# FFN input turned by VectorE instead of TensorE, in a DeltaNet and SwiGLU kernel

## The chip, the cores and the metric

The kernel runs on one NeuronCore of a Trainium2 chip. The core has a matrix engine (TensorE, PE in the profile, with its weight loads as PEld), a vector engine (VectorE, DVE), a scalar engine (ScalarE, ACT), GpSimd (POOL) and SyncE (SP, which here only issues transfers). They run side by side and wait for each other by semaphores. Each engine takes its instructions strictly in the order in which the kernel records them. The metric is the device time in microseconds.

## What is computed

A DeltaNet attention over 4 batches, 8 heads, 768 positions and head size 48 is followed by a SwiGLU feed-forward network (FFN) of 384 to 1536 to 384 channels. All is in fp32; the inputs of the weights come as 64-bit numbers, which the kernel converts itself.

```python
def _attn_ref(q, k, v, beta):
    k_n = k / (np.linalg.norm(k, axis=-1, keepdims=True) + 1e-06)
    for t in range(S):
        y[:, :, t] = np.einsum('bhd,bhde->bhe', q[:, :, t], state)
        v_old = np.einsum('bhde,bhd->bhe', state, kt)
        state = state + bt[:, :, :, None] * np.einsum('bhd,bhe->bhde', kt, vt - v_old)
# bridge: (B,H,S,D) -> (B*S, H*D)
def _moe_ref(x, w_gate, w_val, w_out):
    g = x @ w_gate
    silu = g * (1.0 / (1.0 + np.exp(-g)))
    return (silu * (x @ w_val)) @ w_out
```

## The kernel before

The sequence is cut into 12 chunks of 64 positions. A chunk goes through the recurrence in matrix form (`advance`): with Z, the inverse of a triangular matrix made of K, beta and K, come `p_r`, `p_u` and `uu`, then the new state and Y. Y of a chunk lies in SBUF with two batches times 64 positions on the partitions and, twice (`bp`), 384 channels along the free axis. The FFN's products want the channels on the partitions, so Y is turned into `x_ffn` (`xts[c]`). Before, TensorE does this by six products with the identity and ScalarE copies the result out of PSUM:

```python
        y = work.tile([128, NB, NJ, 2, D], FP32, name="y", tag="r", bufs=2)
        for bp in each:
            nc.scalar.copy(y[:, bp, :, 0], p_y[:, 0, bp])
            for b in range(2):
                nc.scalar.copy(y[half_of(b), bp, :, 1], p_y[half_of(1 - b), 1, bp])
        yield

        y_f = y.rearrange("p bp j par d -> p bp (j par d)")
        xts[c] = ffn_pool.tile([128, KT, TOK], FP32, name="x_ffn")
        p_f = ps_pair("p_f", "py")[:, :, 0 : KT * 128]
        p_f = p_f.rearrange("p bp (t n) -> p t bp n", t=KT)
        for bp in range(NB):
            for t in range(KT):
                at = slice(t * 128, (t + 1) * 128)
                nc.tensor.transpose(p_f[:, t, bp], y_f[:, bp, at], ident)
        x_v = xts[c].rearrange("p t (bp n) -> p t bp n", bp=NB)
        for bp in each:
            nc.scalar.copy(x_v[:, :, bp], p_f[:, :, bp])
        yield
```

The FFN of chunk c runs while the recurrence of chunk c+1 is put between its products. The main loop shows how: `gate_val` makes two of the twelve slices of the FFN's width, `fill(n)` records n further steps of the inversion that yields Z (VectorE's `substitute`, then transposes), and `point(c + 1)` records one step of the recurrence of the next chunk, or the turning of K and Q for a later one. `finish(c + 1)` records what is still left of the next chunk.

```python
        for c in range(2, NCH):
            for f in range(0, FT, 2):
                point(c + 1)
                gate_val(c, f, fill)
            point(c + 1)
            if c >= FAST:
                output_fast(c, fill)
            ...
            finish(c + 1)
```

```python
    def gate_val(c, f, fill, within=None):
        for w_sb, name in ((wg_sb, "p_gate"), (wv_sb, "p_val")):
            ...                       # 6 products of 128x256 into each of two halves
            if name == "p_gate":
                nc.scalar.activation(sil, ps[name], ACTF.Silu)
                fill(2)
        nc.vector.tensor_tensor(out=hs[c, f], in0=sil, in1=ps["p_val"], op=ALU.mult)
        if c >= FAST:
            if f >= FT // 2:
                sums_of_h(c, f)       # three sums or differences of h on VectorE
        fill(3)

    def turned(c, of_q, tag=None):
        ...
        if c >= blocks_of[of_q][1]:   # later chunks of K and Q: VectorE turns 32x32 blocks
            nc.vector.transpose(xt, blocks.rearrange("p bp h d -> p (bp h d)"))
            ...

    def output_fast(c, fill):
        ...                           # the output product in seven block products (chunks 3 to 11)
        product(1, 0, lambda f: h_of(c, f, 1), lambda f: w_t3[:, f])
        add(o[1][:, right], o[0][:, right], p[1, 0])
        fill(2)
        point(c + 1)
        product(0, 0, lambda f: h_of(c, f + FH, 0), quarter(1, 0))
        nc.scalar.copy(o[0][:, left], p[0, 0])
        for f in range(0, FH, 2):
            minus(h_of(c, f + FH, 0), h_of(c, f + FH, 0), s_of(2, f))
        product(1, 1, lambda f: s_of(1, f), lambda f: w_t1[:, f])
        add(o[1][:, right], o[1][:, right], p[1, 1])
        point(c + 1)
        ...                           # product(1, 0) again, then the last one:
        product(1, 1, lambda f: h_of(c, f + FH, 0), quarter(1, 1))
```

In the start, VectorE clears two tiles, the loads follow in the order given here, and the first inversion is made of the diagonal blocks of K's Gram matrix:

```python
        nc.vector.memset(zb, 0.0)
        nc.vector.memset(ztp[0], 0.0)
        ...
        for n in range(4):
            stage(n)                  # pieces of the weights
        load_q(0)
        load_k(2)
        load_k(3)
        ...
        first_diag(1, 0, p_g[1], copy_a)
        r_b = first_n()               # 1 / (norm + 1e-6), from GpSimd's power
        first_diag(1, 1, p_g[1], copy_v)
        nc.vector.transpose(mb.rearrange("p j i -> p (j i)"), first_of["flat"])
```

Of the kernel before, what the change touches and what calls it, by code (L numbers as in the profile page):

```python
# [14 lines left out]
C = 64  # L15
DP = 64
R = 32
# [4 lines left out]
def kernel(  # L22
# [25 lines left out]
    nc = tc.nc  # L48
# [4 lines left out]
    NB = B // 2  # L53
    DM = H * D
    DFF = moe_w_gate.shape[1]
    KT = DM // 128
    FT = DFF // 128
    NG = NCH // 2
    HH = NB * H
# [10 lines left out]
    def ps_pair(name, tag):  # L70

        return psum.tile([128, 2, 512], FP32, name=name, tag=tag, bufs=1)
# [17 lines left out]
    def slot(c):  # L90
        return c if c < AHEAD else (c - AHEAD) % (AHEAD - 1)
# [5 lines left out]
    ident = const.tile([128, 128], FP32, name="ident")  # L97
# [5 lines left out]
    ztp = [const.tile([128, 2, HH, C], FP32, name=f"zt{i}") for i in range(ZB)]  # L103
# [10 lines left out]
    def halves(x, c, bp, b):  # L114
        return x[2 * bp + b, :, c * C : (c + 1) * C, :]
# [9 lines left out]
    def load_q(c):  # L125
        for bp in range(NB):
            for b in range(2):
                nc.sync.dma_start(
                    out=qpad[c % QB][64 * b : 64 * b + 64, bp, :, 0:D],
                    in_=halves(q, c, bp, b).rearrange("h p d -> p h d"),  # L130
                )
# [198 lines left out]
    kt, qt, a_sb, a_of, p_sb, xts = {}, {}, {}, {}, {}, {}  # L330
# [3 lines left out]
    def half_of(x):  # L334
        return slice(64 * x, 64 * x + 64)
# [13 lines left out]
    def norms(c):  # L349

        ksq = work.tile([128, NB, H, D], FP32, name="ksq", tag="r", bufs=2)
        x = knp[c][:, :, :, 0:D]
        nc.vector.tensor_tensor(out=ksq, in0=x, in1=x, op=ALU.mult)
        n = n_t[0][:, c].rearrange("p (par bp j) -> p par bp j", par=2, bp=NB)
        ksq_v = ksq.rearrange("p bp (j par) d -> p par bp j d", par=2)
        for to, of, par in (
            (slice(0, 128), slice(0, 128), 0),
            (half_of(0), half_of(1), 1),
            (half_of(1), half_of(0), 1),
        ):  # L360
            nc.vector.tensor_reduce(
                out=n[to, par], in_=ksq_v[of, par], axis=mybir.AxisListType.X, op=ALU.add
            )
        n = n_t[0][:, c]
        nc.gpsimd.tensor_tensor(out=n, in0=n, in1=half[:, 0:HH], op=ALU.pow)
# [18 lines left out]
    def first_n():  # L384
        n = n_t[0].rearrange("p c h -> p (c h)")
        nc.vector.tensor_scalar_add(n, n, 1e-6)
        r_n = work.tile([128, R], FP32, name="r_n", tag="n_b", bufs=1)
        nc.vector.reciprocal(r_n, n)
        r_b = work.tile([128, R], FP32, name="r_b", tag="nb", bufs=1)
        nc.vector.transpose(r_b, r_n)  # L390
        return r_b
# [135 lines left out]
    def first_tiles():  # L527
        a = work.tile([128, C * 2 * HH], FP32, name="a_sb")

        first_of["flat"] = a[:, 0 : R * R]  # L530
        first_of["diag"] = a[:, 0 : R * R].rearrange("p (j h) -> p h j", j=R)
        a_sb[0] = a[:, R * R :].rearrange("p (c h j) -> p c h j", c=2, h=HH)
        zb = work.tile([128, R, R], FP32, name="zb", bufs=1)
        nc.vector.memset(zb, 0.0)
        nc.vector.memset(ztp[0], 0.0)
        first_of["zb"] = zb

    def first_gram(c, tag):
# [11 lines left out]
    def first_diag(c, par, p, copy):  # L550
        at = HH * c + HH // 2 * par
        copy(first_of["diag"][:, at : at + HH // 2], p[1][:, par, 1])
# [177 lines left out]
    def advance(c):  # L730

        kn = knp[slot(c)]
        zt = ztp[c // 2 % ZB][:, c % 2]
        zt = zt.rearrange("p (par bp j) i -> p par bp j i", par=2, bp=NB)
        if c > 0:
            scale_v(c)
        r = vin.pop(c)
        p_y = recur(ps_pair("p_y", "py"))
        if c > 0:
            p_r = recur(ps_pair("p_r", "px"))  # L740
            for bp, j, par, b, first in every():
                nc.tensor.matmul(  # L742
                    p_r[half_of(b ^ par), par, bp, j],
                    kt[c][half_of(par), bp, j, b],
                    state[half_of(par), b, bp, j],
                    start=first,
                    stop=True,
                    skip_group_check=True,
                )
            for bp, j, par, b, first in every():  # L750
                nc.tensor.matmul(  # L751
                    p_y[half_of(b ^ par), par, bp, j],
                    qt[c][half_of(par), bp, j, b],
                    state[half_of(par), b, bp, j],
                    start=first,
                    stop=False,
                    skip_group_check=True,
                )
            nc.vector.tensor_tensor(out=r, in0=r, in1=p_r, op=ALU.subtract)  # L759
        yield  # L760
        p_u = recur(ps_pair("p_u", "px"))
        for bp, j, par, b, first in every():
            nc.tensor.matmul(  # L763
                p_u[half_of(b), par, bp, j],
                zt[half_of(b ^ par), par, bp, j],
                r[half_of(b ^ par), par, bp, j],
                start=first,
                stop=True,
                skip_group_check=True,
            )  # L770
        uu = work.tile([128, 2, NB, NJ, D], FP32, name="uu", tag="r", bufs=2)
        each = range(NB) if c == 0 else (slice(0, NB),)
        for bp in each:
            nc.scalar.copy(uu[:, :, bp], p_u[:, :, bp])
        if c + 2 < NCH:
            load_v(c + 2)
        yield
        pq = p_sb.pop(c)

        def p_of_u():  # L780
            for bp, j, par, b, first in every():
                nc.tensor.matmul(  # L782
                    p_y[half_of(b ^ par), par, bp, j],
                    pq[half_of(b), par, bp, j],
                    uu[half_of(b), par, bp, j],
                    start=(c == 0 and first),
                    stop=True,
                    skip_group_check=True,
                )

        def of_state():
            p_s = recur(ps_pair("p_s", "px"))
            for bp, j, par, b, first in every():
                nc.tensor.matmul(  # L794
                    p_s[half_of(par), b, bp, j],
                    kn[half_of(b), bp, 2 * j + par],
                    uu[half_of(b), par, bp, j],
                    start=first,
                    stop=True,
                    skip_group_check=True,  # L800
                )
            if c > 0:
                nc.vector.tensor_tensor(out=state, in0=state, in1=p_s, op=ALU.add)
            else:
                nc.scalar.copy(state, p_s)
            for later in range(AHEAD, NCH):
                if freed_by_k(later) == c:
                    load_k(later)

        if 0 < c < NCH - 1:  # L810
            of_state()
        p_of_u()
# [6 lines that stand above are left out]

        y_f = y.rearrange("p bp j par d -> p bp (j par d)")  # L820
        xts[c] = ffn_pool.tile([128, KT, TOK], FP32, name="x_ffn")
        p_f = ps_pair("p_f", "py")[:, :, 0 : KT * 128]
        p_f = p_f.rearrange("p bp (t n) -> p t bp n", t=KT)
        for bp in range(NB):
# [7 lines that stand above are left out]
        if c == 0:  # L832
            of_state()
            yield
# [299 lines left out]
    with tc.manual_schedule(  # L1134
# [14 lines left out]

        nc.vector.memset(places[0][:, 0:1], 0)  # L1150
        norms(1)
        for n in range(4):
            stage(n)
        load_q(0)
        load_k(2)
        load_k(3)
        for n in range(4, 10):
# [5 lines left out]
        copy_a, copy_v = nc.scalar.copy, nc.vector.tensor_copy  # L1163
        turned(0, False)
        turned(1, False, "py")
        p_g = [first_gram(0, "px"), first_gram(1, "py")]
        first_diag(0, 0, p_g[0], copy_a)
        first_diag(0, 1, p_g[0], copy_v)
        copy_a(beta_b, beta_s.rearrange("p (g r) -> p g r", g=NG)[:, :, 0:R])
        first_diag(1, 0, p_g[1], copy_a)  # L1170
        r_b = first_n()
        first_diag(1, 1, p_g[1], copy_v)
        mb = new_mb()
        nc.vector.transpose(
            mb.rearrange("p j i -> p (j i)"), first_of["flat"]
# [121 lines left out]
```

## Time and profile before

The time before is 738.33 us, the median of three runs (738.02 to 739.34). The profiled execution spans 737.5 us.

| row of the profile | count | busy us | mean ns of one |
|---|---|---|---|
| L847 products `p_gate` and `p_val` | 1728 | 204.4 + 198.5 | 387 and 379 |
| L959 and L876 products `p_o` | 900 | 182.8 | 326 to 499 |
| L827 transposes `p_f` of Y | 72 | 10.6 | 286 |
| L830 copies `x_ffn` of 128x768 | 11 | 8.8 | 798 |
| L510 and L516 substitution | 372 | 63.3 + 63.7 | 340 and 343 |
| L862 `h_f` | 71 | 48.6 | 684 |
| L422 turning of K and Q by VectorE | 15 | 18.3 | 1216 to 1240 |

A line such as `L862 DVE ...` names the source line, the engine, the operation, what it writes and what it reads, with partitions x elements. In the timeline the first number is the start in us, the second the length. The chain of waits follows the work that ended last back to the start and gives, for each piece, its start and length. The busy time of an engine says how long its instructions ran, not whether something waited for them.

### The profile page before, as it was taken

The page shows a single profiled execution, that of the slowest core. Times are in us where ns is not written, and L with a number is a line of the kernel's source. Part 1 is how long each engine was busy: PE and PEld are TensorE (multiplying, and loading weights), DVE is VectorE, ACT ScalarE, POOL GpSimd, SP SyncE. Part 2 cuts the span into 40 slices and gives each one's busy share as a digit, 9 for nine tenths or more (in the row PEclk, how much of TensorE's full clock was granted, in tenths as well). Part 3 has the DMA queues.
Part 4 walks back from the last instruction along what each step waited for, and adds up shares of the span by engine and source line. Part 5 has one row for each costly group of instructions (what it writes and reads, how often), then busy time and mean ns, then how long its engine had stood idle before and what let it go on. Part 6 is the DMA issues. An engine that isn't in the chain of part 4 may idle for free.

```text
span 737.5 us, 22478 instructions
## 1 busy us (share of the span) xinstructions
PE 697.5 (95%) x10132; PEld 604.7 (82%) x10132; DVE 473.1 (64%) x977; ACT 154.7 (21%) x287; POOL 66.9 (9%) x46
## 2 busy tenths in 40 slices
PE   4657899999999999999999999999999999999997
PEld 3546788866787788988988988988988988989987
DVE  5999988978498163678854678854578853313122
ACT  3455443302401112011012011012011012021010
POOL 7008100201200000030000030000030000000000
PEclk9556999999999999999999999999999999999999
DMA  6775444121231012331302231302210100100000
GB/s 141 164 227 166 124 108 129 36 41 24 56 45 24 22 24 45 43 67 15 53 3 45 36 70 20 53 3 39 46 29 12 32 3 3 23 3 0 22 1 21
DMA packets 130735, 37.18 MB, mean 50 GB/s; under 512 B 122864, under 2 KB 125936, under 8 KB 130640
## 3 DMA queue, kind: packets, MB, share of 16 engines
q1 hardware_dynamic: 127184, 34.01, 22.7%
q10 hardware_dynamic: 3072, 1.57, 1.0%
q8 instruction: 79, 1.29, 0.7%
q0 software_dynamic: 384, 0.17, 0.1%
q14 instruction: 16, 0.13, 0.1%
HBM read 31.01 MB, written 4.72 MB: 48 GB/s over the span
## 4 chain that ended last, share of the span: by engine, by line
PE 83%; DVE 14%; issue 1%; DMA 1%; ACT 0%; ACTq 0%; SPq 0%; DVEq 0%
PE p_gate L847 23%; PE p_val L847 23%; PE p_o L959 17%; PE p_o L876 6%; DVE tmp L510 3%; PE p_g L444 3%; DVE zb L516 3%; PE p_u L763 2%; PE p_r L742 1%; PE p_s L794 1%; PE p_y L782 1%; PE p_y L751 1%; DVE last_h L287 1%; PE p_t L432 1%; DVE h_f L862 1%
## 5 line engine op out<-in xcount | busy, mean ns | idle before, releaser
L847 PE MATMUL p_gate<-x_ffn,wg_sb 128*128 128x256 f32 x864 | 204.4, 387 | 1.5 <-ACT x_ffn L830 1.5
L847 PE MATMUL p_val<-x_ffn,wv_sb 128*128 128x256 f32 x864 | 198.5, 379 | 0.0
L847 PEld LDWEIGHTS p_val<-x_ffn,wv_sb 128*128 128x128 f32 x864 | 163.8, 190 | 22.3
L847 PEld LDWEIGHTS p_gate<-x_ffn,wg_sb 128*128 128x128 f32 x864 | 161.1, 191 | 24.2 <-ACT x_ffn L830 2.0
L862 DVE TENSOR_TENSOR h_f<-sil,p_val 128x512 f32<-128x512 f32 x71 | 48.6, 684 | 147.5 <-PE p_val L847 147.0
L856 ACT ACTIVATE sil<-p_gate 128x512 f32<-128x512 f32 x72 | 43.0, 598 | 276.9 <-PE p_gate L847 247.3
L655 POOL TENSOR_TENSOR n_b<-mb,half 128x32 f32<-128x32 f32 x5 | 43.0, 8607 | 408.6 <-DVE mb L480 368.2
L959 PE MATMUL p_o<-wo_sb,h_f 128*128 128x192 f32 x432 | 75.6, 328 | 0.1
L959 PEld LDWEIGHTS p_o<-wo_sb,h_f 128*128 128x128 f32 x432 | 70.3, 190 | 1.2 <-DVE o_sb L969 0.7
L510 DVE TENSOR_TENSOR tmp<-zb,mb 128x31 f32<-128x31 f32 (+15 forms) x186 | 63.3, 340 | 12.2 <-PE p_j L630 6.8
L516 DVE TENSOR_TENSOR zb<-zb,tmp 128x31 f32<-128x31 f32 (+15 forms) x186 | 63.7, 343 | 6.5 <-DVE tmp L510 0.2
L969 DVE TENSOR_TENSOR o_sb<-o_sb,p_o 128x192 f32<-128x192 f32 x45 | 15.8, 350 | 53.4 <-PE p_o L959 36.2
L876 PE MATMUL p_o<-wo_sb,h_f 128*128 128x384 f32 x136 | 45.7, 490 | 0.0
L876 PEld LDWEIGHTS p_o<-wo_sb,h_f 128*128 128x128 f32 x136 | 25.3, 190 | 16.5
L959 PE MATMUL p_o<-last_k,h_f 128*128 128x192 f32 x180 | 32.2, 326 | 0.0
L959 PEld LDWEIGHTS p_o<-last_k,h_f 128*128 128x128 f32 x180 | 29.7, 190 | 0.0
L917 DVE TENSOR_TENSOR h_f<-h_f,h_f 128x256 f32<-128x256 f32 x54 | 22.4, 424 | 8.0 <-PE p_o L959 7.1
L959 PE MATMUL p_o<-last_h,h_f 128*128 128x192 f32 x144 | 26.3, 326 | 0.0
L959 PEld LDWEIGHTS p_o<-last_h,h_f 128*128 128x128 f32 x144 | 23.9, 190 | 0.0
L254 ACT ACTIVATE last_h<-last_h,rebias 128x512 int32<-128x512 uint32 (+2 forms) x26 | 15.3, 616 | 30.5 <-DVE last_h L246 30.4
L763 PEld LDWEIGHTS p_u<-vin,zt 64*64 64x64 f32 x768 | 13.7, 141 | 6.9 <-issue 3.2
L763 PE MATMUL p_u<-vin,zt 64*64 64x48 f32 x768 | 15.7, 228 | 2.4 <-DVE vin L759 1.2
(180 smaller groups left out, 692.6 us busy)
## 6 DMA issues: line engine op xcount, KB each, us to landing
vin<-in_v_dram SPq DMA_DIRECT2D x96, 48.0 KB
kn<-in_k_dram SPq DMA_DIRECT2D x40, 96.0 KB
out_dram<-o_sb SPq DMA_DIRECT2D x36, 96.0 KB
zt<-in_moe_w_out_dram SPq DMA_DIRECT2D x6, 384.0 KB
staged<-in_moe_w_out_dram SPq DMA_DIRECT2D x6, 384.0 KB
qpad<-in_q_dram SPq DMA_DIRECT2D x36, 64.0 KB
wo_sb<-in_moe_w_gate_dram SPq DMA_DIRECT2D x4, 512.0 KB
wo_sb<-in_moe_w_val_dram SPq DMA_DIRECT2D x4, 512.0 KB
```

The lines of the kernel that those rows point to most:

```text
L444: nc.tensor.matmul(p_v[par][half_of(b if of_q else b ^ par), bp, j], kt[c][half_of(par), bp, j, b], xt[half_of(par), bp, j, b],)
L510: nc.vector.tensor_tensor(out=t_v, in0=zb[:, 0 : j + 1, j : j + 1].to_broadcast([128, j + 1, m]), in1=mb[:, j : j + 1, j + 1 : R].to_broad ...
L516: nc.vector.tensor_tensor(out=zb[:, 0 : j + 1, j + 1 : R], in0=zb[:, 0 : j + 1, j + 1 : R], in1=t_v, op=ALU.add,)
L655: nc.gpsimd.tensor_tensor(out=n, in0=mb.rearrange("p j i -> p (j i)")[:, 0 : R * R : R + 1], in1=half, op=ALU.pow,)
L763: nc.tensor.matmul(p_u[half_of(b), par, bp, j], zt[half_of(b ^ par), par, bp, j], r[half_of(b ^ par), par, bp, j], start=first, stop=True, ...
L847: nc.tensor.matmul(ps[name][:, i], w_sb[:, t, (f + i) * 128 : (f + i + 1) * 128], xts[c][:, t], start=(t == 0), stop=(t == KT - 1),)
L856: nc.scalar.activation(sil, ps[name], ACTF.Silu)
L862: nc.vector.tensor_tensor(out=hs[c, f], in0=sil, in1=ps["p_val"], op=ALU.mult)
L876: nc.tensor.matmul(p_o, hs[c, f - f % 2][:, f % 2, bp * 128 : (bp + 1) * 128], wo_sb[:, f], start=(f == 0), stop=(f == FT - 1),)
L917: nc.vector.tensor_tensor(out=out, in0=a, in1=b, op=ALU.subtract)
L959: nc.tensor.matmul(p[x, part], a(f - f % 2)[:, f % 2], b(f), start=not begun and f == 0, stop=f == FH - 1, skip_group_check=True,)
L969: nc.vector.tensor_tensor(out=out, in0=a, in1=b, op=ALU.add)
```

## The change

From chunk 2 on, Y is turned by VectorE's transpose of 32x32 blocks straight from SBUF to SBUF: sixteen instructions per chunk, each taking 32 partitions of Y to 32 partitions of `x_ffn`. TensorE's six transposes, ScalarE's copy and the PSUM tile between them go away for these ten chunks. The aim is to take work from TensorE. The input needs no further step in between, as the loop over the 4 x 4 blocks does the exchange of the block rows.

Two smaller parts come with it. Z's first tile is cleared by ScalarE, which multiplies a repeated identity by zero, instead of VectorE's memset; and Q's first loads are issued ahead of the first four weight pieces. Besides, the second diagonal copy of VectorE is recorded ahead of the norm's steps.

```diff
         nc.vector.memset(zb, 0.0)
-        nc.vector.memset(ztp[0], 0.0)
+        nc.scalar.mul(
+            ztp[0].rearrange("p c h i -> p (c h i)").rearrange("p (n i) -> p n i", i=128),
+            ident[:, None, :].to_broadcast([128, 2 * HH * C // 128, 128]),
+            0.0,
+        )
...
         xts[c] = ffn_pool.tile([128, KT, TOK], FP32, name="x_ffn")
+        if c > 1:
+
+            y_q = y_f.rearrange("p bp (t q d) -> p q t bp d", t=KT, q=4)
+            x_q = xts[c].rearrange("p t (bp q n) -> p q t bp n", bp=NB, q=4)
+            for of_x in range(4):
+                for of_y in range(4):
+                    nc.vector.transpose(
+                        x_q[R * of_x : R * of_x + R, of_y],
+                        y_q[R * of_y : R * of_y + R, of_x],
+                    )
+            yield
+            return
         p_f = ps_pair("p_f", "py")[:, :, 0 : KT * 128]
...
         norms(1)
+        load_q(0)
         for n in range(4):
             stage(n)
-        load_q(0)
         load_k(2)
...
         first_diag(1, 0, p_g[1], copy_a)
+        first_diag(1, 1, p_g[1], copy_v)
         r_b = first_n()
-        first_diag(1, 1, p_g[1], copy_v)
         mb = new_mb()
```

## The prediction

> **What bounds the kernel now.** I read the page's shares and slices first, then the chain that ended last, then the timeline around each place where Y becomes the FFN's input x.
>
> ```profile
> PE 697.5 (95%) x10132; PEld 604.7 (82%) x10132; DVE 473.1 (64%) x977; ACT 154.7 (21%) x287; POOL 66.9 (9%) x46
> ...
> PE 83%; DVE 14%; issue 1%; DMA 1%; ACT 0%; ACTq 0%; SPq 0%; DVEq 0%
> ```
>
> TensorE bounds it. VectorE's 64% looks like room, but the share is an average. Before about 90 us VectorE carries the chain, and later it comes back in three short pieces. Here is the chain of work around one of them:
>
> ```profile
> 334.31 0.70 DVE h_f L862
> ...
> 338.70 0.42 DVE tmp L510
> ...
> 344.87 1.26 DVE kt L422
> 346.12 0.04 issue
> 346.17 1.16 PE p_g L444 x64
> ```
>
> From 334.31 to 346.12 the chain runs on VectorE without a hole (11.27 us busy of 11.90 by the window sums), and TensorE stands before `p_g` until `kt` is turned. The same stretch is on the chain at 445.4 to 457.2 and, ending in `qt`, at 556.5 to 568.3.
>
> What the change removes from TensorE is seen in the timeline near 408 us:
>
> ```profile
> 407.99 0.82 PE L827 MATMUL p_f<-ident,y 128*128 128x128 f32 x6
> 408.64 4.07 PE L959 MATMUL p_o<-wo_sb,h_f 128*128 128x192 f32 x24
> ```
>
> From the start of `p_f` to the start of the next product is 0.65 us: that is the price of the six transposes, not the 0.82 of their records, which overlap. Ten chunks make 6.5 us, the most that TensorE can gain.
>
> And the one x that is awaited (chunk 2), in the timeline:
>
> ```profile
> 191.78 0.80 ACT L830 COPY x_ffn<-p_f 128x768 f32<-128x768 f32 x1 [1.38 <-PE p_f L827]
> ...
> 192.63 2.86 PE L847 MATMUL p_gate<-x_ffn,wg_sb 128*128 128x256 f32 x12 [0.52 <-ACT x_ffn L830]
> ...
> 193.04 0.28 DVE L516 TENSOR_TENSOR zb<-zb,tmp 128x112 f32<-128x112 f32 x1
> ```
>
> **What the new instructions cost.** Their nearest kin in the groups by shape and the timeline:
>
> ```profile
> L688 DVE STREAM_TRANSPOSE z<-zt 32x256 f32<-32x256 f32 x16 | 6.1, 415 | 0.2
> L665 DVE STREAM_TRANSPOSE n_t<-n_b 128x32 f32<-128x32 f32 x5 | 1.1, 212 | 0.2
> ```
>
> [...] So a full turn of Y takes 4 x 4 instructions, each on 32 partitions and 192 elements (six blocks), and a quarter of the lanes. [...] the four L688 of one group start at 373.76, 374.13, 374.54 and 374.91, and the next instruction at 375.33. Where the quadrant stays, the step is 0.37 us; where it changes, 0.41 to 0.43, and nothing overlaps. In the new loop the input's quadrant changes at every instruction, so all are held. From 32 elements (212 ns) to 256 (433 ns for the held one) is 0.99 ns per element; 192 elements are 212 + 160 x 0.99 = 370 ns, plus 14 ns between two held ones, 0.385 us. Sixteen make **6.15 us of VectorE per chunk**, 61 us in all, against 0.65 us of TensorE and 0.80 us of ScalarE (L830) removed per chunk.
>
> **The change part by part.** In the built program's order the sixteen stand where the generator's step stands, so each place is worked out by itself.
>
> Chunk 2. They follow the substitution step that ends at 193.32 (L516 above), so x is ready at 193.32 + 6.15 + 0.1 = 199.55 where it was 192.58. The first `p_gate` waits for all sixteen: +6.95 us, all on the path.
>
> Chunk 3. y is ready at 235.6, VectorE is free from 241.8 and idle for 15.3 us up to 257.07, and x is needed at 251.5. Hidden; -0.65 us.
>
> Chunks 5, 7, 9. The sixteen stand between the substitution steps at 338.26 and 338.70, inside the stretch where VectorE is the chain. Everything behind shifts by 6.15 us: `kt` ends at 352.3 instead of 346.1, TensorE stands before `p_g`, and its 0.65 us come back as a longer wait. +6.15 us each, 18.45 us.
>
> Chunks 4, 6, 8. They start after the `o_sb` sum at 297.15 (chunk 4), at 297.5, and end at 303.65. Three differences of h (L917), which the last product reads, come next; TensorE, 0.65 us earlier, would reach that product at 302.81 and now waits for the first difference until about 304.15. `kt` then ends at 306.4 and `qt` at 307.5, against 303.2 and 304.3. The second `p_g` starts at 307.6 instead of 306.5, and `p_gate` at 308.65 instead of 307.52: +1.1 us each, 3.3 us.
>
> Chunk 10 has only `qt` to turn; the same reckoning from 629.2 gives +1.0 us. Chunk 11 (664 us): VectorE idles 5.8, 5.8 and 3.9 us before the `h_f` around it, so it has caught up before the `h_f` of 675.17; hidden, -0.65 us.
>
> The start. Z's clearing (1.76 us of VectorE at 2.45) is followed by 2.62 us of waiting for k, so its removal gains nothing; ScalarE has room between its table load (ends 4.9) and 7.97. Q's loads in front of the weights end TensorE's 2.36 us wait for `qpad` at 19.1, but VectorE's substitution is the path there. What matters is TensorE's stop in the middle of the first `p_g`, which the chain shows as
>
> ```profile
> 12.96 2.90 issue
> ```
>
> The trace doesn't say what it waits for. DMA share is 0.99 in that window, with the four weight pieces just issued. [...] If Q ahead of the weights shortens it, the norm's power on GpSimd (ends 16.17) becomes the limit and about 1.0 us is gained. If it stays, the 0.8 us of norm work that now stand behind the second diagonal copy go on the path. I take -0.3.
>
> Sum: 6.95 - 0.65 + 18.45 + 3.3 + 1.0 - 0.65 - 0.3 = **+28.1 us**, of which nothing is given back later, as TensorE bounds what lies between.
>
> The clock comes on top. In chunks 2, 5, 7, 9 TensorE now stands idle for some 7.4 to 8 us. [...] in windows of 3.41 us:
>
> ```profile
> 12.72:16.13 3.41, 0.51 (x54) 0.34 (x43) 0.57 (x1) 0.35 (x1) 3.41 (x2) 1.00 0.99 277
> 16.13:19.54 3.41, 1.05 (x46) 0.83 (x24) 2.83 (x7) 2.69 (x5) 0.79 (x4) 0.50 0.70 101
> 26.37:29.78 3.41, 3.41 (x125) 3.30 (x128) 3.13 (x9) 1.07 (x2) 0.00 (x0) 0.50 1.04 339
> 29.78:33.19 3.41, 1.21 (x79) 1.07 (x72) 3.17 (x8) 1.07 (x2) 0.00 (x0) 1.00 0.52 95
> ```
>
> The second number is TensorE's busy time, the one before the DMA share its granted clock: 0.51 us busy is followed by half clock, a full window by full clock. A stop of over 6.8 us holds one whole window. Half clock then lasts for the rest of the window of the restart (1.7 us on average) and one full window, 5.1 us, which costs half of that, 2.6 us. Four stops make 10 us; I take 8, since a small-tile window may count otherwise.
>
> 738.3 + 28.1 + 8 = **774 us**.
>
> **Rivals.** First: TensorE is the bound at 95% and VectorE has 36% free, so 6.5 us are gained, about 731 us. The shares speak for it; against it speaks the chain, which has VectorE at exactly the places where three of the ten blocks of sixteen land, and the awaited x of chunk 2. Second: the transposes overlap each other, as records of equal quadrants do, and cost 0.25 to 0.3 us, 4.5 us per chunk. Then chunk 2 costs 5.3, the three odd ones 13.5, the even ones give 0.5 each back: some +15 us, with the clock 760. Third: the stops come without the clock's fall[...]: 766.
>
> **Range and chances.** 757 to 785 holds the second and third rivals and a clock loss twice as large. Slower by over 2% begins at 753.1, just under the range: 0.91. Within 2% needs transposes of about 4 us and no clock loss: 0.06. Faster by over 2% (under 723.6) is more than removing all the transposes could give: 0.03.
>
> **What will show it.** Right: 160 transposes of 32x192 with a mean near 370 ns and steps near 0.385; VectorE near 530 us busy; waits of TensorE for `x_ffn` of some 7 us once and for `kt` or `qt` of 7 to 8 us three times, a new wait for h of about 1.3 us at the even chunks; slices of PEclk under 9 after 190, 350, 460 and 570 us. Wrong: steps under 0.3 us, `p_g` of chunk 5 less than 5 us later relative to the `p_val` before it, or a first `p_gate` of chunk 2 that doesn't wait for VectorE.

## The result, and the profile after

The changed kernel takes 779.15 us, the median of four runs (776.65 to 781.21), where the kernel before took 738.61 (738.02 to 739.34; the three runs of the first part and one more). The ratio is 1.0547, with a 95% interval of 1.0507 to 1.0586: slower. The profiled execution is the 776.65; it spans 774.9 us, 37.4 more than the one of before.

The page of the kernel after: busy times, the granted clock in slices, the shares of the chain that ended last, and the group of the new instructions.

```profile
PE 697.8 (90%) x10072; PEld 604.6 (78%) x10072; DVE 528.5 (68%) x1136; ACT 148.5 (19%) x278; POOL 67.7 (9%) x46
...
PEclk9657999999799999997999999999999899999999
...
PE 70%; DVE 25%; issue 2%; POOL 1%; DMA 1%; SPq 0%; DVEq 0%; ACT 0%
...
L832 DVE STREAM_TRANSPOSE x_ffn<-y 32x192 f32<-32x192 f32 x160 | 59.1, 369 | 2.0
```

TensorE has 60 products fewer and is busy for as long as before (697.8 against 697.5 us), because some of its products ran at half clock. Past the start the PEclk row shows it as two sevens and an 8 (chunks 2, 5 and 9); in chunk 7 the half clock lies across two slices, and both still show a 9. VectorE gained 55 us of work, and its part of the chain rose from 14% to 25%. TensorE's waits from 150 us to the end name the places (total us, times, longest):

```profile
PE p_g L444 <- DVE kt L422: 15.4, 3, 7.6
PE p_o L975 <- DVE o_sb L985: 8.1, 4, 2.0
PE p_g L444 <- DVE qt L422: 7.6, 1, 7.6
PE p_gate L863 <- DVE x_ffn L832: 7.3, 1, 7.3
```

There is one wait for x, in chunk 2, and there are four for an `o_sb` sum, one in each of chunks 4, 6, 8 and 10. Of the four for `kt` and `qt`, three are 7.6 us long (15.4 + 7.6 is three times 7.6 plus a remainder of 0.2); those belong to chunks 5, 7 and 9. The timeline of the kernel after in chunk 2 and in chunk 5 (start, length, and in brackets the wait of the first product):

```profile
192.78 6.11 DVE L832 STREAM_TRANSPOSE x_ffn<-y 32x192 f32<-32x192 f32 x16
198.94 5.39 PE L863 MATMUL p_gate<-x_ffn,wg_sb 128*128 128x256 f32 x12 [7.30 <-DVE x_ffn L832]
...
348.71 6.11 DVE L832 STREAM_TRANSPOSE x_ffn<-y 32x192 f32<-32x192 f32 x16
361.03 1.25 DVE L422 STREAM_TRANSPOSE kt<-qpad 128x1024 f32<-128x1024 f32 x1
362.33 1.99 PE L444 MATMUL p_g<-kt 64*64 64x64 f32 x64 [7.63 <-DVE kt L422]
```

Sixteen transposes take 6.11 us. Behind each stop the products run slowly: these twelve took 2.86 us before and take 5.39, and these 64 took 1.16 and take 1.99. The granted clock around chunk 2, in stretches of 3.41 us laid on the clock's steps (length, busy time of PE, PEld, DVE, ACT and POOL, granted clock, DMA share, GB/s):

```profile
190.45:193.86 3.41, 0.75 (x64) 0.64 (x64) 3.14 (x12) 1.63 (x3) 0.00 (x0) 1.00 0.77 158
193.86:197.27 3.41, 0.00 (x0) 0.00 (x0) 3.29 (x10) 0.00 (x0) 0.00 (x0) 0.50 0.20 37
197.27:200.68 3.41, 1.74 (x4) 1.47 (x5) 1.57 (x5) 0.00 (x0) 0.00 (x0) 0.50 0.00 0
200.68:204.10 3.42, 3.42 (x9) 2.71 (x9) 0.00 (x0) 0.00 (x0) 0.00 (x0) 0.50 0.00 0
204.10:207.51 3.41, 3.41 (x64) 2.79 (x64) 0.00 (x0) 0.60 (x1) 0.00 (x0) 1.00 0.00 0
```

To see where the 37.4 us arose, I compared the starts of the 72 `silu` activations (six per chunk) in the two traces. The table gives what each chunk lost or gained in all (+ is later than before); the clock's part is what the products behind a stop took beyond their former time.

| place | us | of which clock |
|---|---|---|
| start | -0.55 | |
| chunk 2 | +9.39, and +0.33 at its fourth pair of products | 2.53 |
| chunk 3 | -0.66 | |
| chunks 4, 6, 8, 10 | +1.62 each | |
| chunks 5, 7, 9 | +7.99, +7.38, +7.66 | 1.95, 1.35, 1.63 |
| chunk 11 | -0.66 | |
| sum | 37.4 | 7.46 |

### The profile page after: what moved, and what is told of

Its sections match the earlier page's. It is cut to its first block, busy times and chain, and to the rows that moved or that the text cites. A ratio compares the mean times of both kernels' runs of the same rounds, so it can differ in the third digit from the quotient of the medians.

```text
span 774.9 us, 22499 instructions
## 1 busy us (share of the span) xinstructions
PE 697.8 (90%) x10072; PEld 604.6 (78%) x10072; DVE 528.5 (68%) x1136; ACT 148.5 (19%) x278; POOL 67.7 (9%) x46
## 4 chain that ended last, share of the span: by engine, by line
PE 70%; DVE 25%; issue 2%; POOL 1%; DMA 1%; SPq 0%; DVEq 0%; ACT 0%
PE p_gate L863 22%; PE p_val L863 21%; PE p_o L975 13%; DVE x_ffn L832 6%; DVE tmp L510 4%; DVE zb L516 4%; PE p_g L444 3%; PE p_o L892 2%; PE p_u L767 1%; PE p_r L746 1%; PE p_s L798 1%; PE p_y L786 1%; PE p_y L755 1%; DVE h_f L933 1%; DVE h_f L878 1%
## 5 line engine op out<-in xcount | busy, mean ns | idle before, releaser
L863 PE MATMUL p_gate<-x_ffn,wg_sb 128*128 128x256 f32 x864 | 207.7, 391 | 8.2 <-DVE x_ffn L832 7.3
L863 PEld LDWEIGHTS p_gate<-x_ffn,wg_sb 128*128 128x128 f32 x864 | 163.6, 194 | 32.0 <-DVE x_ffn L832 7.4
L975 PE MATMUL p_o<-wo_sb,h_f 128*128 128x192 f32 x432 | 78.0, 335 | 8.1 <-DVE o_sb L985 8.1
L975 PEld LDWEIGHTS p_o<-wo_sb,h_f 128*128 128x128 f32 x432 | 72.7, 195 | 9.9 <-DVE o_sb L985 9.2
L510 DVE TENSOR_TENSOR tmp<-zb,mb 128x31 f32<-128x31 f32 (+15 forms) x186 | 63.3, 340 | 15.4 <-PE p_j L634 10.1
L832 DVE STREAM_TRANSPOSE x_ffn<-y 32x192 f32<-32x192 f32 x160 | 59.1, 369 | 2.0
L892 PEld LDWEIGHTS p_o<-wo_sb,h_f 128*128 128x128 f32 x136 | 25.4, 190 | 16.7
L444 PE MATMUL p_g<-kt 64*64 64x64 f32 x576 | 12.0, 241 | 15.4 <-DVE kt L422 15.4
L444 PEld LDWEIGHTS p_g<-kt 64*64 64x64 f32 x576 | 10.8, 154 | 18.0 <-DVE kt L422 16.6
```

Source lines behind the costliest of these rows:

```text
L444: nc.tensor.matmul(p_v[par][half_of(b if of_q else b ^ par), bp, j], kt[c][half_of(par), bp, j, b], xt[half_of(par), bp, j, b],)
L510: nc.vector.tensor_tensor(out=t_v, in0=zb[:, 0 : j + 1, j : j + 1].to_broadcast([128, j + 1, m]), in1=mb[:, j : j + 1, j + 1 : R].to_broad ...
L832: nc.vector.transpose(x_q[R * of_x : R * of_x + R, of_y], y_q[R * of_y : R * of_y + R, of_x],)
L863: nc.tensor.matmul(ps[name][:, i], w_sb[:, t, (f + i) * 128 : (f + i + 1) * 128], xts[c][:, t], start=(t == 0), stop=(t == KT - 1),)
L892: nc.tensor.matmul(p_o, hs[c, f - f % 2][:, f % 2, bp * 128 : (bp + 1) * 128], wo_sb[:, f], start=(f == 0), stop=(f == FT - 1),)
L975: nc.tensor.matmul(p[x, part], a(f - f % 2)[:, f % 2], b(f), start=not begun and f == 0, stop=f == FH - 1, skip_group_check=True,)
```

## The experiments

The theory: the sixteen cost what they take because each one waits for the one before; they cost time only where VectorE is the chain or x is awaited; and the long stops lower TensorE's clock besides. The rivals: the clock falls for another cause, the steps have nothing to do with the partitions read and written, or the smaller parts of the change carry some of the loss. All kernels are the changed kernel with the edit shown, so all of them hold the start's parts too. A set of chunks in an edit means that the others keep TensorE's transposes.

### Each place by itself

The start's parts alone, with Y turned by TensorE everywhere:

```diff
-        if c > 1:
+        if False:
```

> The changed kernel with Y turned by TensorE in all chunks again; only the parts at the start are kept (Q's loads ahead of the weights, Z cleared by ScalarE, the order of the second diagonal copy). Theory (the loss is VectorE's transposes, the start gives a little): the first silu comes 0.5 us earlier than before and nothing else moves, 738.6 - 0.55 = 738.0 us. Rival (the start parts carry a good part of the 40 us, for instance by late weights): over 745 us. Rival (the start gives the most of what was meant): under 735 us.

739.53 us in 13 runs, ratio 1.0005 [0.9997, 1.0013], where 738.0 was expected. The -0.55 of the two traces doesn't stand out from the scatter of the start: in the thirteen traces of kernels with this same start, the last `silu` of chunk 1 comes 0.08 to 1.15 us earlier than in the one trace of before. Clearing Z by ScalarE and loading Q ahead make no difference that the 13 runs show.

Only chunks 3 and 11:

```diff
-        if c > 1:
+        if c in (3, 11):
```

> VectorE turns Y in chunks 3 and 11 alone, the two where VectorE idles; start parts kept. Theory (what a transpose block costs depends on what stands behind it on VectorE): 0.66 us gained in each, 738.0 - 1.3 = 736.7 us, no half clock after 70 us. Rival (sixteen VectorE instructions cost their 6.1 us wherever they stand): 738.0 + 12.2 - 1.3 = 749 us.

737.63 us in 19 runs, ratio 0.9979 [0.9972, 0.9986]. In the trace, -0.65 and -0.66 us: where VectorE idles, the whole price of TensorE's six transposes is gained.

Only chunks 5, 7 and 9:

```diff
-        if c > 1:
+        if c in (5, 7, 9):
```

> VectorE turns Y in chunks 5, 7 and 9 alone, at the place of the changed kernel; start parts kept. Theory: three stops of TensorE before p_g, 6.0 us each without the clock and 1.3 to 2.6 us by half clock after each, 738.0 + 18.1 + 4 to 8 = 760 to 764 us. Rival (chunk 2 and the even chunks make most of the loss): under 750 us.

762.14 us, ratio 1.0317 [1.0301, 1.0332], inside the expected 760 to 764. The three chunks lose 6.88, 7.57 and 8.55 us, so the mechanism needs none of the other places. The clock's part (0.84, 1.53 and 2.51 once 6.04 is taken off) differs from that in the changed kernel (1.95, 1.35 and 1.63); the stops lie otherwise against the stretches of 3.41 us, which I take for the cause.

Only chunks 4, 6, 8 and 10:

```diff
-        if c > 1:
+        if c in (4, 6, 8, 10):
```

> VectorE turns Y in chunks 4, 6, 8 and 10 alone, at the place of the changed kernel; start parts kept. Theory: 1.62 us lost in each as in the changed kernel's trace, no half clock, 738.9 + 6.5 = 745.4 us. Rival (the loss of the even chunks comes only with the stops of the odd ones around them): about 736 us.

748.03 us (745.56 to 748.89), ratio 1.0118 [1.0101, 1.0136], 2.6 above what was expected. The profiled execution, the 745.56, has +1.62 or +1.63 in chunks 6, 8 and 10 and +2.76 in chunk 4. There, TensorE stands 1.18 us ahead of `p_gate`, and the profile gives no releaser ("issue"). The other three runs are 2 to 3 us longer and left no trace, so what they lost is open.

### What the even chunks wait for

I had predicted a wait for the first difference of h. The timeline of the kernel after, chunk 4:

```profile
305.93 6.11 DVE L832 STREAM_TRANSPOSE x_ffn<-y 32x192 f32<-32x192 f32 x16
...
312.07 1.10 DVE L933 TENSOR_TENSOR h_f<-h_f,h_f 128x256 f32<-128x256 f32 x3
313.09 0.35 DVE L985 TENSOR_TENSOR o_sb<-o_sb,p_o 128x192 f32<-128x192 f32 x1
313.49 2.22 PE L975 MATMUL p_o<-wo_sb,h_f 128*128 128x192 f32 x12 [2.01 <-DVE o_sb L985]
```

Before, the same sum and the same product stood so:

```profile
301.71 0.35 DVE L969 TENSOR_TENSOR o_sb<-o_sb,p_o 128x192 f32<-128x192 f32 x1 [1.52 <-PE p_o L959]
...
303.46 2.11 PE L959 MATMUL p_o<-wo_sb,h_f 128*128 128x192 f32 x12
```

The sum was over 1.4 us ahead of the product. Now the product starts when the sum behind the three differences ends: it accumulates in the PSUM tile `p[1, 1]`, which that sum reads. VectorE runs transposes, differences and sum in the order in which the kernel records them (305.93, 312.07, 313.09). So in the even chunks I recorded the sum first:

```diff
+        sum_first = c + 1 in (4, 6, 8, 10)
-        for f in range(0, FH, 2):
+        for f in () if sum_first else range(0, FH, 2):
             minus(h_of(c, f + FH, 0), h_of(c, f + FH, 0), s_of(2, f))
         product(1, 1, lambda f: s_of(1, f), lambda f: w_t1[:, f])
         add(o[1][:, right], o[1][:, right], p[1, 1])
+        for f in range(0, FH, 2) if sum_first else ():
+            minus(h_of(c, f + FH, 0), h_of(c, f + FH, 0), s_of(2, f))
```

> As the run with chunks 4, 6, 8 and 10 alone, but there the sum of o_sb is recorded ahead of the three differences of h. Theory (the last product waits for the o_sb sum, which reads the PSUM tile that this product goes on filling): TensorE starts it 0.6 us earlier, 1.0 lost in each, 738.9 + 4.0 = 743 us. Rival (the prediction's reading: it waits for the first difference of h): the sum ahead of it delays it by 0.35 us, 738.9 + 7.9 = 747 us.

743.93 us, ratio 1.0068 [1.0054, 1.0082]. Chunks 6, 8 and 10 lose 0.93, 0.93 and 0.94 us where they lost 1.62; chunk 4 loses 2.21, with a stop of 1.3 us by "issue" in the same place as in the run before. In the waits of this kernel the sum has given way to h:

```profile
PE p_o L975 <- DVE h_f L933: 5.3, 4, 1.3
```

The wait of 1.3 us that I had predicted is there once the sum doesn't stand behind the differences. The sum's place explains 0.69 of the 1.62 us; the rest stays, as the sixteen are still ahead of the first difference.

### What makes a step of 0.38 us

In the trace of before, the steps of the L688 transposes are 0.37 us while the quarter of the partitions (the quadrant of the prediction) stays, and 0.41 to 0.43 where it changes. At the change in the middle of the four, from 374.13 to 374.54, the quarter that is read and the one that is written change together, so that trace doesn't tell which of the two counts. The changed loop changes the input's quarter at each instruction, and the output's at every fourth. One edit keeps each transpose within its own quarter (this leaves out the exchange of the block rows, so x is another matrix), the other only exchanges the loops, which leaves x as it was:

```diff
                         x_q[R * of_x : R * of_x + R, of_y],
-                        y_q[R * of_y : R * of_y + R, of_x],
+                        y_q[R * of_x : R * of_x + R, of_y],
```

> The changed kernel with the same 160 transposes of 32x192, but each from a quarter of the partitions into the same quarter, and the quarter changes only at every fourth one; the exchange of the block rows is left out, so x is another matrix. The theory (an instruction whose quarter differs from that of the one before waits for it to end) expects 12 of 16 steps near 0.30 us and 4 near 0.385, some 5.15 us per chunk instead of 6.11, and 0.95 us less in each of chunks 2 and 4 to 10: about 771 us. The rival (the steps are as long as the instruction, whatever its quarter) expects 6.1 us per chunk and 779 us.

```diff
-            for of_x in range(4):
-                for of_y in range(4):
+            for of_y in range(4):
+                for of_x in range(4):
```

> The changed kernel with the two loops over the block rows exchanged and nothing else: the quarter that is read stays for four transposes, while the quarter that is written changes at every one. If only the quarter that is read holds an instruction back, the sixteen take 4.6 us as in the run where each stayed in its own quarter, and the time is that run's 764 us. If the quarter that is written does it too, they take 6.1 us and the time stays at 779 us.

Within its own quarter: 764.37 us, ratio 1.035 [1.0336, 1.0364]. With the loops exchanged: 776.84 us (776.01 to 781.22), ratio 1.053 [1.0505, 1.0555], an interval that overlaps that of the changed kernel. The sixteen of chunk 2 in the first of them, from its timeline:

```profile
192.50 4.63 DVE L832 STREAM_TRANSPOSE x_ffn<-y 32x192 f32<-32x192 f32 x16
```

and the group of all 160 in the second:

```profile
L832 DVE STREAM_TRANSPOSE x_ffn<-y 32x192 f32<-32x192 f32 x160 | 59.0, 369 | 2.0
```

A change of either quarter lengthens the step. With reading and writing in one quarter the steps are 0.26 us (the one behind a change 0.30), and the next begins some 65 ns before the last ends; at a change the step is 0.34 us and the next begins 13 ns after. With the loops exchanged, only the written quarter changes at twelve of the fifteen steps, and they are 0.37 to 0.39 us like the rest, as in the changed kernel. It is the change that counts, and not that a block goes from one quarter into another: two L688 transposes of the kernel before do that too, from the same quarter into the same other one, and there the second starts 0.37 us after the first, which takes 0.43. The sixteen of a full turn of Y are sixteen different pairs of quarters, so any two that follow each other differ in one of the two; the two orders of the loops that were run take 59.1 and 59.0 us for all 160. My expectation for the first kernel, 771, took steps of 0.30; it gains 1.48 us per chunk (6.11 - 4.63) and not 0.95, in chunks 2, 5, 7 and 9 and about as much in the four even ones, some 12 us, which is what the two spans differ by (774.9 and 762.7).

A kernel with four transposes over all 128 partitions, which leaves out the same exchange, shows how much less is lost when the turn is short:

```diff
-            for of_x in range(4):
-                for of_y in range(4):
-                    nc.vector.transpose(
-                        x_q[R * of_x : R * of_x + R, of_y],
-                        y_q[R * of_y : R * of_y + R, of_x],
-                    )
+            for of_y in range(4):
+                nc.vector.transpose(x_q[:, of_y], y_q[:, of_y])
```

> The changed kernel with four transposes of 128x192 per chunk in place of sixteen of 32x192. The exchange of the block rows between quadrants is left out, so x is not the reference's; the same elements are read and written. Theory (VectorE's time is set by the number of instructions, since each works on a quarter of the lanes): 1.3 us per chunk instead of 6.1; chunk 2 costs 2.0, chunks 5, 7, 9 1.3 each, chunks 3, 4, 6, 8, 10, 11 give 0.66 each: 738.9 + 1.9 = 741 us, no half clock after 70 us. Rival (the amount of data turned sets the time, or TensorE waits for x as such): over 765 us.

743.8 us, ratio 1.0068 [1.0055, 1.0082], 2.8 above what was expected. Four transposes take 1.15 us, the even chunks and 3 and 11 gain 0.66 each, the odd ones lose 1.69, 1.82 and 2.42, and chunk 2 loses 3.44 where I had expected 2.0. I had expected no loss of clock from stops this short, and there is some (below): in chunk 2 the first twelve products take 4.54 us in place of 2.86, which is 1.68 of its 3.44.

### Whether the stops lower the clock

If TensorE's idling lowers its clock, then products that nobody reads, put into the stops, must keep it up and must lower the time although they add work. Two kernels differ in the counts alone (29 and 32, then 14 and 16):

```diff
+    def keep_busy(p, n):
+        for _ in range(n):
+            nc.tensor.matmul(p[:, 0:256], wg_sb[:, 0, 0:128], wg_sb[:, 0, 0:256])
...
+        if idle:                                  # ahead of p_g, chunks 5, 7, 9
+            keep_busy(p_g[0], idle.pop())         # 32, then 16
...
+            if c == 2 and f == 0 and name == "p_gate":
+                keep_busy(ps[name][:, 0], 29)     # then 14
```

> The changed kernel, with products of weights that nobody reads put where TensorE stands idle: 29 of 128x256 in front of chunk 2's first p_gate, 32 in front of the first p_g after x of chunks 5, 7 and 9 (0.216 us each, so 6.3 and 6.9 us, inside stops of 6.9 and 7.6 us; they write the same PSUM tile, which the real products then overwrite). Theory (half clock after each stop costs 7.5 us in all in the profiled run): no half clock after 70 us, the same stops end at the same instructions, 779.15 - 7.5 = 771.6 us, and the runs scatter less than 776.65 to 781.21. Rival (the stops' length is the whole loss): 779 us.

794.71 us, ratio 1.0749 [1.0733, 1.0766]: a miss, whose time says nothing about the dispute. One such fp32 call is two recorded products and takes 0.43 us, so the fillings took 14.5 (partly at half clock) and 14.0 us in stops of 7.3 and 7.6, and TensorE was late by itself.

> The changed kernel, with products that nobody reads put into TensorE's four long stops of chunks 2, 5, 7 and 9: 14 calls (28 recorded products) ahead of p_gate and 16 calls (32) ahead of each p_g, at 0.43 us a call 6.0 and 6.9 us, which fits into stops of 7.3 and 7.6 us. The theory (the clock falls because TensorE stands idle) expects no half clock after 70 us, the same waits for x_ffn and kt shrunk to about 1 us, and 771.6 us, 7.5 under the changed kernel. The rival (the clock falls for another reason, or the lost time belongs to the waits themselves) expects 779 us and half clock at the same four places.

774.1 us, ratio 1.0474 [1.0459, 1.0488]. The granted clock of this kernel, in slices:

```profile
PEclk8657999999999999999999999999999999999999
```

The four falls are gone. Set beside before, chunks 2, 5, 7 and 9 lose 6.79, 6.04, 6.02 and 5.92 us instead of 9.39, 7.99, 7.38 and 7.66: 7.65 us less. TensorE still waits for x and for `kt` or `qt` at the end of the fillings (0.97 us once, 0.7 three times), so the stall itself has stayed. That part of the expectation held. The expectation of no half clock at all failed at one place, chunk 6 (below). The medians differ by 5.05 us and the two profiled executions (776.65 and 771.83) by 4.8, not by 7.5, for two losses that are not in the changed kernel's trace took 3.3 us of the gain back: 1.73 in chunk 2, with a stop of 1.52 us by "issue", whose cause the trace doesn't give, and 1.6 in chunk 6, where half clock followed a stop of 2.01 us.

### A version that gains

Where VectorE idles, the change gains. The even chunks have such room too, but ahead of the output's last sums and not after them, and in several pieces. This kernel uses VectorE in chunks 3, 4, 6, 8, 10 and 11, leaves 2, 5, 7 and 9 to TensorE, and cuts the sixteen of an even chunk into 8, 3 and 5, recorded ahead of two of the sums and at the next step of the recurrence:

```diff
+        if c in (4, 6, 8, 10):
+            blocks_for_x(c, y)        # lists the sixteen, records none
+            yield
+            turn_blocks(16)           # what is left of them
+            yield
+            return
...
-        if c > 1:
+        if c in (3, 11):
...
+        turn_blocks(8)
         add(o[0][:, right], o[0][:, right], p[0, 1])
...
+        turn_blocks(3)
         add(o[1][:, right], o[0][:, right], p[1, 0])
```

> VectorE turns Y in chunks 3, 4, 6, 8, 10, 11; in the even ones the sixteen are cut into 8, 3 and 5 and stand ahead of the output sums, where VectorE waited for TensorE (3.3 and 1.5 us before). Chunks 2, 5, 7, 9 stay with TensorE. Theory: all hidden, 0.66 us gained in six chunks, 738.0 - 4.0 = 734.1 us, below both kernels. Rival (the even chunks lose 1.6 us by the amount of VectorE work, not by its place): 738.0 - 1.3 + 4 x 1.6 = 743 us.

734.5 us (734.09 to 735.11), ratio 0.9941 [0.9928, 0.9953]: 0.6% below before, a small gain, but one whose interval stays clear of 1. Its timeline in chunk 4:

```profile
290.26 3.03 DVE L738 STREAM_TRANSPOSE x_ffn<-y 32x192 f32<-32x192 f32 x8 [0.16 <-ACT y L842]
...
293.77 1.14 DVE L738 STREAM_TRANSPOSE x_ffn<-y 32x192 f32<-32x192 f32 x3
...
295.67 1.91 DVE L738 STREAM_TRANSPOSE x_ffn<-y 32x192 f32<-32x192 f32 x5
```

The last one ends at 297.58, and each of the six chunks gains 0.66 us. The same kernel with its loops exchanged (the edit shown above):

> The split kernel (VectorE in chunks 3, 4, 6, 8, 10 and 11, the even ones cut into 8, 3 and 5 ahead of the output sums) with the loops exchanged in the same way. Its transposes lay in VectorE's idle time already, so shorter ones gain nothing there: 734.5 us by both theories. A lower time would say that a part of them was still on TensorE's path.

734.44 us, ratio 0.9943 [0.9929, 0.9957]: the same time as without the exchange. Its profiled execution is the longest of the five, 736.1: in chunk 2, up to which the two programs are the same, half clock came in it and not in the other's, and its first `silu` falls 1.77 us behind.

## Why the prediction was right, step by step

The prediction was 774.0 us with a range of 757 to 785, and "slower". The measured 779.15 lies in the range, 5.2 above the middle.

- **A step of 0.385 us, 6.15 us per chunk**: held. The steps are 0.38, the mean is 369 ns, sixteen take 6.11.
- **Chunk 2, +6.95**: held. 6.86 without the clock, and 0.33 three pairs of slices later: there VectorE starts to turn K 1.43 us after the start of the last `silu` (218.29 and 216.86) where it was 1.11 before (209.13 and 208.02), with 0.24 us of idling ahead for which the trace gives no releaser.
- **Chunks 3 and 11, hidden, -0.65**: held, in the changed kernel and alone.
- **Chunks 5, 7, 9, +6.15**: held. Without the clock the net loss is 6.04 each. The 0.66 gained first is given back: TensorE reaches `p_g` earlier and waits longer.
- **Chunks 4, 6, 8, +1.1, and 10, +1.0**: mis-sized. Each lost 1.62, 2.2 us more in all. The step that failed is "now waits for the first difference of h". TensorE waited for the sum of `o_sb`, which VectorE reaches 1.0 us later, behind all three differences. Recording it ahead of them moved the loss from 1.62 to 0.93. The predicted end of that path, a wait for `qt` at the second `p_g`, isn't there either: behind the product TensorE waits for nothing more, so the loss is the stop of 2.01 less the 0.66 saved, and some 0.27 more until the next product.
- **The start, -0.3**: nothing measurable.
- **The clock, +8**: held as a term, 7.46 in the profiled execution and 7.65 by the products put into the stops. The 2.6 us per stop was an estimate from the stretches of 3.41 us in the trace of before; in chunk 2 half clock covered 1.74 + 3.42 us of products and cost 2.53 us, in chunks 5, 7 and 9 it cost 1.35 to 1.95. But the reason given for the size, "a stop of over 6.8 us holds one whole window", asked for too much: stops of 2.0 to 2.5 us were followed by half clock too, where they left 0.89 to 1.40 us of products in one stretch of 3.41 (last section). The third rival, no clock loss, falls.
- **The first and second rivals** fall too: the transposes don't overlap, and VectorE's free third lay elsewhere.

The terms above make 37.4 us in the profiled execution where I had 28.1 + 8 = 36.1 (2.2 more for the even chunks, 0.9 less for the rest); a median of 40.5 above before is 3 us more. The profiled execution is the shortest of the four, and no trace was left by the others. The kernel with even chunks alone has the same scatter of 2 to 3 us. Half clock behind a stop of 2.01 us cost 1.6 us, and it came behind three of twenty such stops (last section), so two more of them would make the difference. That isn't shown: the mean granted clocks of the four, 0.949, 0.951, 0.945 and 0.947 in the order 776.65, 780.81, 777.5 and 781.21, include the start and don't follow the times.

## What to carry to other kernels

A free share of an engine is a sum over stages: look at each place where the moved work would land, and at what stands behind it in that engine's order. Here 6 us of VectorE cost nothing in two chunks, 1.6 us in four, and 7 to 9 us in four, the clock's part included; moving only what fits the holes, and cutting it to their size, turned a loss of 5.5% into a gain of 0.6%. When work is put in front of an engine that feeds TensorE, count the clock that the stop costs as a term of its own, here 7.46 of 37.4 us.

## What was not expected of the hardware

**Short stops lower the clock too.** In the kernel with four wide transposes TensorE stands 2.31 us ahead of `p_gate`; the stretch that holds most of this stop, and the next:

```profile
191.08:194.49 3.41, 1.10 (x28) 0.91 (x16) 2.33 (x9) 1.40 (x3) 0.00 (x0) 1.00 0.80 172
194.49:197.90 3.41, 3.41 (x10) 2.70 (x9) 0.00 (x0) 0.00 (x0) 0.00 (x0) 0.50 0.01 2
```

The same follows stretches with 1.25, 0.89 and 0.90 us of products ahead of chunks 5, 7 and 9 of that kernel. None of these stretches was wholly idle.

The clearest case is the stop of 2.01 us ahead of the last output product of an even chunk. It stands in five of the traces (the changed kernel, the one with its loops exchanged, the one with even chunks alone and the two with fillings), twenty times in all; what differs is its place against the stretches. Here it is in chunk 6 of the kernel with the shorter fillings (428.86 to 430.87), with the stretch behind it, and then in chunk 8 of the changed kernel (552.20 to 554.21):

```profile
428.16:431.57 3.41, 1.40 (x9) 1.11 (x8) 3.34 (x9) 0.00 (x0) 0.00 (x0) 1.00 0.00 0
431.57:434.99 3.42, 3.42 (x34) 2.98 (x36) 2.12 (x4) 0.00 (x0) 0.00 (x0) 0.50 0.37 52
...
552.26:555.67 3.41, 1.46 (x9) 1.46 (x10) 3.37 (x8) 0.00 (x0) 0.00 (x0) 1.00 0.00 0
555.67:559.09 3.42, 3.42 (x136) 3.08 (x135) 2.86 (x6) 0.00 (x0) 0.00 (x0) 1.00 0.31 44
```

The first stop lies wholly within one stretch, which leaves 1.40 us of products in it, and half clock follows. The second began 0.06 us ahead of the stretch, 1.46 us are left, and full clock stays. So it is with all twenty: three lay within one stretch (the other two in chunks 4 and 8 of the kernel with the longer fillings), and half clock followed each; seventeen reached across the border of two, and it followed none of them. In the three cases the chunk lost 3.20 to 3.30 us in place of 1.62.

The 1.40 and the 1.46 us out of 3.41 were measured in stretches that hold products with 128x128 weights alone. Where many small ones are among them, busy time didn't decide: half clock followed 2.19 us in chunk 2 of the split kernel with its loops exchanged, and full clock 1.98 us in the same place of the kernel with four wide transposes.

The stretches lie on a fixed grid: in each of the fourteen traces all changes of the granted clock are whole multiples of 3.413 us apart, wherever the stops lie. In the changed kernel these changes lie, from 193.86 us to 606.87, 10.24, 153.60, 10.24, 112.64, 6.83, 112.64 and 6.83 us apart, which is 3, 45, 3, 33, 2, 33 and 2 times 3.413. So one and the same stop of 2.01 us, at the same instruction, cost no clock in the trace of one kernel and 1.6 us in that of another.

**The written quarter holds an instruction back as the read one does.** The kernel before showed steps of 0.37 and 0.41 to 0.43 us for its 32x256 transposes; the two edits of the loop put the difference at 0.26 us against 0.38 for 32x192.
